# Two MLPs behind a Fourier transform: other steps give their squares and low parts to VectorE

## Chip, cores and metric

One core of a Trainium2 chip runs the whole program. The metric is the device time of one execution in microseconds (us). The kernel before was timed in 3 runs: median 1021.49 us, 1020.7 to 1024.02.

## The reference

```
X = fft(fft(x, axis=1), axis=2).real          # x: 2 x 3008 x 256
x = X.reshape(6016, 256)
h = x @ w_in;  g = relu(h) ** 2;  x = g @ w_out             # 256 -> 2048 -> 256
h = x @ w_in2; g = h * sigmoid(1.702 * h); out = g @ w_out2 # 256 -> 2048 -> 256
```

All inputs are float32. A float32 matrix product is made from three products of TensorE: each operand is split into a high part (a cast to the type fp32r) and a low part (the operand less its high part), and high x high, high x low and low x high are summed in PSUM.

## The kernel before, in words

The transform is folded by symmetry, so that the tokens come as 8 blocks (2 batches x 4 sets of frequencies) of 376 or 378 pairs; a pair is a frequency and its mirror. The features lie on the partitions. Names for the engines: PE is TensorE, DVE VectorE, ACT ScalarE, POOL GpSimd, SP the queue that issues all DMAs.

**The first MLP runs in 128 steps** (`steps`, the loop `for i in range(n)`). A step is one block and one group of 128 of the 2048 hidden features, and has these parts:

- `front1` (L468 to L470): 6 matmuls of 376 or 378 columns on TensorE into two PSUM tiles `psa`, an even and an odd part. Each of the two tiles has two buffers, so a step needs the tiles that were used two steps earlier.
- VectorE reads them: L727 makes `p` (even part plus a rank-one term), L729 and L730 make the two halves of `h`, sum and difference. L727 frees the even tile, L730 the odd one.
- the square of the relu of `h` (752 or 756 columns), in place. In a step of the set `SV` VectorE does it in one operation (L734); in any other step ScalarE does it in two, relu (L736) and square (L737).
- ScalarE casts `h` to its high part `gh` (L739).
- the low part `gl = h - gh`, a line of a helper (L76), one step later in the program: by VectorE if the step is in the set `VSTEPS`, else by GpSimd. `h` has 4 buffers, shared with the staging tiles `o` of outputs; `gh` and `gl` have 5.
- `back` (L483), four steps later (`LAG`): 12 matmuls from `gh`, `gl` and the output weights into two accumulators `psb`. At the end of a turn (4, 8 or 16 steps of a block) two copies (L596, one on ScalarE, one on VectorE) empty them into `o`, and a DMA stores it.

**Beside these, `background(i)` puts pieces of other work behind each step**, by the table `PLAN` (start, rate, due step): the weights of the first MLP are prepared (`conv`, up to step 36), further blocks of the transform folded, those of the second MLP prepared (`w2a`, steps 55 to 78, and `w2b`, 85 to 117), and the second MLP's first input read back (`y0`, from step 117). A group of weights (`widen`, `widen_in`, `narrow`) is turned from 64-bit words into float32 by L169 and L172 on ScalarE and L173, L174, L182, L183 and L185 on VectorE; ScalarE casts it (L208, L254), and VectorE or GpSimd (L76, and L246 for sums of the second MLP's) makes its low part. L173 needs L169, L183 needs L172 (or L182). L293 to L311 fold blocks of the transform. L620 adds parts of the second MLP's input on GpSimd.

**The order on each engine** is fixed when the program is built: a scheduler goes through the program with its own estimate of times and issues each engine's instructions in the order in which it expects them to be ready. Each engine then runs its list strictly in order and waits on semaphores. So a change of who makes a square moves other instructions too.

**The second MLP** (from `with tc.manual_schedule()`) is ordered by hand, in 64 units, and takes the second half of the time.

Of the kernel before, what the change touches and what calls it, by code (L numbers as in the profile page):

```python
# [42 lines left out]
THROTTLE = 18  # L43

LOW = {(0, 0, 0): "V", (0, 0, 1): "V", (0, 0, 2): "G", (0, 0, 3): "G", (0, 1, 0): "G", (0, 1, 1): "G", (0, 1, 2): "G", (0, 1, 3): "V", (1, 0, 0): "G", (1, 0, 1): "G", (1, 0, 2): "G", (1, 0, 3): "G", (1, 1, 0): "G", (1, 1, 1): "G", (1, 1, 2): "G", (1, 1, 3): "V"}
VSTEPS = {17, 23, 26, 28, 29, 34, 44, 45, 50, 60, 75, 76, 82, 89, 113}
RA = {(0, 0, 0), (0, 0, 1), (0, 0, 2), (0, 0, 3), (0, 1, 1), (0, 1, 2), (0, 1, 3), (1, 0, 1)}
EOG = {1, 2, 3}
SV = {3, 9, 13, 17, 19, 25, 34, 49, 51, 79, 80, 96}
LOWE = {(0, 0): "V", (0, 1): "G", (0, 2): "V", (0, 3): "V", (1, 0): "V", (1, 1): "G", (1, 2): "G", (1, 3): "V"}  # L50
FINE = set()
PARKED = ((0, 2), (1, 2), (0, 3), (1, 3))
# [11 lines left out]
def spectral_two_mlps_kernel(  # L64
# [10 lines left out]
    def sub(eng, o, a, b):  # L75
        eng.tensor_tensor(out=o, in0=a, in1=f32(b), op=ALU.subtract)  # L76
# [511 lines left out]
    def store(j, f):  # L588

        wd = WID[blocks[j][1]]  # L590
        y = dram.tile([P, 2, 2, NP], F32, tag=f"y{j}_{f}", name="ydram")
        ydram.setdefault(j, []).append(y)
        for ec in range(2):
            o = m.tile([P, 2, NP], F32, tag="h", name="o", bufs=4)
            ap = acc[j][ec][:, :, 0:wd]
            (A.copy, V.tensor_copy)[ec](o[:, :, 0:wd], ap)  # L596
            nc.sync.dma_start(y[:, ec, :, 0:wd], o[:, :, 0:wd])
# [103 lines left out]
    for i in range(n):  # L701
# [29 lines left out]
        if done and done[3]:  # L731
            store(*done[:2])
        if i in SV:
            V.scalar_tensor_tensor(out=hv, in0=hv, scalar=0.0, in1=hv, op0=ALU.max, op1=ALU.mult)  # L734
# [6 lines left out]
        def low_part(i, key, h, gh):  # L741
            pw = WID[blocks[key[0]][1]]
            gl = mg.tile([P, 2, NP], F32R, tag="gl", name="gl", bufs=5)
            sub(G if i not in VSTEPS else V, gl[:, :, 0:pw], h[:, :, 0:pw], gh[:, :, 0:pw])
            gst[key] = (gh, gl)
# [270 lines left out]
```

## Time and profile before

| | |
|---|---|
| median of 3 runs | 1021.49 us |
| the profiled execution: its time, its span | 1022.03 us, 1020.2 us |
| TensorE (PE) busy | 983.7 us, 96% |
| VectorE (DVE) busy | 816.6 us, 80% |
| ScalarE (ACT) busy | 612.9 us, 60% |
| GpSimd (POOL) busy | 354.6 us, 35% |
| relu (L736), square (L737), cast (L739) on ScalarE, mean of one | 832, 834, 821 ns |
| granted clock of TensorE, mean | 0.99 |

The span runs from the first instruction to the last. Busy shares are means over stages with different limits, so they are read by stretches. A busy TensorE is not at its peak: the ends of its matmuls are modelled, and they overlap (one takes 0.34 us and the next starts 0.17 us after it). The granted clock is the share of TensorE's full 2.4 GHz that it got. A number in brackets behind a row of the order of time is the engine's idle time before the row, with the instruction whose end released it.

### The profile page before, as it was taken

The numbers are of one execution on the slowest core, as the hardware profiler recorded it, in microseconds if no ns is written. First come the engines' busy times: TensorE is split into PE (matmuls) and PEld (weight loads), VectorE is DVE, ScalarE is ACT, GpSimd is POOL, SyncE is SP. The second block draws the span as 40 slices with busy tenths as digits, with TensorE's granted clock in tenths as the row PEclk, the third lists the DMA queues.
The fourth block names the chain that finished last, engine by engine and source line by source line (L and its number), as shares of the span: only waits on it lengthen the run. The fifth ranks groups of instructions, "written<-read, shape, count | busy, mean of one in ns | idle before, by whom it ended". The sixth has DMA issues, their size and how long they took to land.

```text
span 1020.2 us, 14245 instructions
## 1 busy us (share of the span) xinstructions
PE 983.7 (96%) x5582; PEld 948.6 (93%) x5582; DVE 816.6 (80%) x1089; ACT 612.9 (60%) x764; POOL 354.6 (35%) x216
## 2 busy tenths in 40 slices
PE   9989989899999999998899999999999999999998
PEld 9579978898999898898899999999999999999997
DVE  7996899885777598775678888888888888888874
ACT  2577666775888588687744454544545454454443
POOL 2447554643867449596605302002020020200000
PEclk9899999999999999899999999999999999999999
DMA  7531221201233021201441200000100000000000
GB/s 293 208 119 71 73 85 70 72 31 54 104 124 114 31 83 57 73 16 61 186 132 31 77 16 31 31 32 16 46 1 31 31 31 31 1 31 1 31 1 30
DMA packets 22914, 65.22 MB, mean 64 GB/s; under 512 B 1856, under 2 KB 14272, under 8 KB 19648
## 3 DMA queue, kind: packets, MB, share of 16 engines
q1 hardware_dynamic: 22848, 64.32, 17.7%
q8 instruction: 43, 0.70, 0.3%
q14 instruction: 23, 0.19, 0.1%
HBM read 43.13 MB, written 21.19 MB: 63 GB/s over the span
## 4 chain that ended last, share of the span: by engine, by line
PE 69%; DVE 16%; ACT 7%; issue 5%; POOL 1%; DMA 0%; DVEq 0%; ACTq 0%; POOLq 0%
PE psb L796 24%; PE psc L780 21%; PE psb L483 13%; PE psa L468 2%; PE psa L367 2%; ACT h L736 2%; PE psa L469 2%; PE psa L470 2%; DVE h L730 2%; DVE p L727 2%; DVE h L729 2%; ACT h L737 2%; DVE ue L183 1%; DVE gl L76 1%; PE psa L284 1%
## 5 line engine op out<-in xcount | busy, mean ns | idle before, releaser
L76 POOL TENSOR_TENSOR gl<-h,gh 128x752 fp32r<-128x752 f32 (+1 forms) x113 | 218.5, 1944 | 157.9 <-ACT gh L739 135.7
L483 PE MATMUL psb<-gh,w 128*128 128x376 f32 (+1 forms) x1024 | 241.6, 338 | 4.3 <-DVE o L596 4.3
L796 PE MATMUL psb<-gh,w 128*128 128x376 f32 (+1 forms) x1024 | 237.8, 334 | 0.0
L483 PEld LDWEIGHTS psb<-gh,w 128*128 128x128 f32 x1024 | 184.8, 191 | 6.0 <-DVE o L596 5.5
L796 PEld LDWEIGHTS psb<-gh,w 128*128 128x128 f32 x1024 | 182.9, 188 | 0.0
L736 ACT ACTIVATE h<-h 128x752 f32<-128x752 f32 (+1 forms) x116 | 96.2, 832 | 81.0 <-DVE h L730 75.8
L483 PE MATMUL psb<-gl,w 128*128 128x376 f32 (+1 forms) x512 | 132.2, 339 | 2.2 <-POOL gl L76 2.2
L861 ACT ACTIVATE g<-c 128x1128 f32<-128x1128 f32 (+1 forms) x64 | 73.7, 1152 | 99.5 <-DVE c L859 99.5
L796 PE MATMUL psb<-gl,w 128*128 128x376 f32 (+1 forms) x512 | 129.9, 335 | 0.4 <-DVE gl L76 0.3
L739 ACT CAST gh<-h 128x752 fp32r<-128x752 f32 (+1 forms) x128 | 104.7, 821 | 23.3 <-DVE h L734 16.2
L76 DVE TENSOR_TENSOR gl<-g,gh 128x1504 fp32r<-128x1504 f32 (+1 forms) x64 | 111.8, 1747 | 1.6 <-ACT gh L841 1.6
L630 POOL TENSOR_TENSOR ue<-raw 128x376 f32<-128x376 f32 (+1 forms) x16 | 18.4, 1174 | 271.4 <-DVE ya L76 271.2
L841 ACT CAST gh<-g 128x1504 fp32r<-128x1504 f32 (+1 forms) x64 | 93.1, 1454 | 31.4 <-DVE g L832 31.4
L727 DVE SCALAR_TENSOR_TENSOR p<-n,w1n_t,psa 128x376 f32<-128x376 f32 (+1 forms) x128 | 76.0, 600 | 41.6 <-PE psa L470 41.2
L468 PE MATMUL psa<-eo,w 128*128 128x376 f32 (+1 forms) x256 | 90.5, 355 | 16.9 <-DVE h L730 11.6
L737 ACT ACTIVATE h<-h 128x752 f32<-128x752 f32 (+1 forms) x116 | 96.4, 834 | 3.0
L483 PEld LDWEIGHTS psb<-gl,w 128*128 128x128 f32 x512 | 94.0, 191 | 2.5 <-POOL gl L76 2.5
L796 PEld LDWEIGHTS psb<-gl,w 128*128 128x128 f32 x512 | 92.1, 188 | 1.0 <-DVE gl L76 1.0
L832 DVE TENSOR_TENSOR g<-g,c 128x1128 f32<-128x1128 f32 (+1 forms) x64 | 89.8, 1403 | 1.2 <-ACT g L861 1.2
L858 DVE TENSOR_TENSOR g<-g,psc 128x376 f32<-128x376 f32 (+1 forms) x64 | 35.0, 547 | 69.0 <-ACT g L857 69.0
L469 PE MATMUL psa<-eo,w 128*128 128x376 f32 (+1 forms) x256 | 86.1, 337 | 0.0
L470 PE MATMUL psa<-eo,w 128*128 128x376 f32 (+1 forms) x256 | 85.8, 336 | 0.0
(139 smaller groups left out, 1625.6 us busy)
## 6 DMA issues: line engine op xcount, KB each, us to landing
ydram<-o SPq DMA_DIRECT2D x18, 376.0 KB, 2.9
xt<-in_x SPq DMA_DIRECT2D x5, 1024.0 KB, 6.9
cst<-in_dfts SPq DMA_DIRECT2D x8, 570.0 KB, 6.0
raw<-ydram SPq DMA_DIRECT2D x6, 752.0 KB, 4.6
out<-o SPq DMA_DIRECT2D x11, 376.0 KB, 3.1
raw<-in_w1i SPq DMA_DIRECT2D x4, 1024.0 KB, 5.4
raw<-in_w1o SPq DMA_DIRECT2D x4, 1024.0 KB, 6.5
raw<-in_w2i SPq DMA_DIRECT2D x4, 1024.0 KB, 4.9
```

The costliest lines, as they stand in the source:

```text
L76: eng.tensor_tensor(out=o, in0=a, in1=f32(b), op=ALU.subtract)
L468: T.matmul(o, lhsT=w[:, 0, fs], rhs=t[:, par, 0, 0:wd], start=True, stop=False)
L469: T.matmul(o, lhsT=w[:, 0, fs], rhs=t[:, par, 1, 0:wd], start=False, stop=False)
L470: T.matmul(o, lhsT=w[:, 1, fs], rhs=t[:, par, 0, 0:wd], start=False, stop=True)
L483: T.matmul(acc[j][ec][:, s, 0:wd], lhsT=w[:, hl, e0:e0 + P], rhs=(gh, gl)[gi][:, s, 0:wd], start=(first and hl == 0 and gi == 0), stop=(la ...
L727: V.scalar_tensor_tensor(out=p[:, 0:wd], in0=e128[blocks[j]][:, 0:wd], scalar=w1n_t[:, 0, f:f + 1], in1=ps[:, 0, 0:wd], op0=ALU.mult, op1= ...
L736: A.activation(out=hv, in_=hv, func=AF.Relu)
L737: A.activation(out=hv, in_=hv, func=AF.Square)
L739: last_a = A.copy(gh[:, :, 0:wd], hv)
L780: T.matmul(bank, lhsT=w[:, hl, slot * P:(slot + 1) * P], rhs=t[:, yl, i], start=(first and hl == 0 and yl == 0), stop=(hl == 1), skip_grou ...
L796: T.matmul(o[:, s, 0:wd], lhsT=w[:, hl, e0:e0 + P], rhs=g[:, 2 * i + s, 0:wd], start=(f == 0 and hl == 0 and g is gh), stop=(f == 15 and h ...
L841: A.copy(gh[:, :, 0:pw], g[:, :, 0:pw])
```

## The change

Two sets of step numbers are replaced. `SV`, the steps whose square VectorE makes, had 12 members and has 15; `VSTEPS`, those whose low part VectorE makes, had 15 and has 12. Up to step 43 both are now empty. Nothing else is edited.

```diff
-VSTEPS = {17, 23, 26, 28, 29, 34, 44, 45, 50, 60, 75, 76, 82, 89, 113}
+VSTEPS = {44, 45, 50, 58, 61, 72, 75, 82, 93, 96, 107, 110}
-SV = {3, 9, 13, 17, 19, 25, 34, 49, 51, 79, 80, 96}
+SV = {49, 51, 59, 60, 66, 73, 74, 79, 80, 94, 95, 101, 108, 109, 115}
```

The scheduler then orders the engines anew. Pieces of these orders follow, from steps 24 to 31 on three engines and from steps 115 to 118 on one. The numbers behind names tell tiles apart and differ between the two programs.

TensorE at step 30. The first row is the last front matmul of step 29; `psb` rows are the output matmuls of step 24, `psa_1392` (before) and `psa_1398` (changed) the even tile of step 30, `psa_1435` that of step 31. Before:

```order
L470 MATMUL psa_1345<-eo_304,w_871 128x378
L483 MATMUL psb_1352<-gh_1210,w_727 128x378 x2
L483 MATMUL psb_1352<-gl_1246,w_727 128x378 x2
L483 MATMUL psb_1352<-gh_1210,w_727 128x378 x2
L483 MATMUL psb_1353<-gh_1210,w_727 128x378 x2
L483 MATMUL psb_1353<-gl_1246,w_727 128x378 x2
L483 MATMUL psb_1353<-gh_1210,w_727 128x378 x2
```

With the change:

```order
L470 MATMUL psa_1351<-eo_304,w_874 128x378
L468 MATMUL psa_1398<-eo_304,w_874 128x378
L469 MATMUL psa_1398<-eo_304,w_874 128x378
L470 MATMUL psa_1398<-eo_304,w_874 128x378
L468 MATMUL psa_1435<-eo_304,w_874 128x378
L483 MATMUL psb_1358<-gh_1215,w_729 128x378 x2
L483 MATMUL psb_1358<-gl_1252,w_729 128x378 x2
```

Four front matmuls, of steps 30 and 31, now stand ahead of the output matmuls of step 24.

ScalarE in the same place, from the cast of the weights before (L208) to the first operations on the next weights (L169, L172). `h_1238` and `h_1269` are steps 25 and 26 before, `h_1243` and `h_1275` the same with the change. Before:

```order
L208 CAST w_1214<-ue_1114 128x1024
L739 CAST gh_1244<-h_1238 128x756
L736 ACTIVATE h_1269<-h_1269 128x756
L596 COPY o_1309<-psb_1077 128x2x376
L737 ACTIVATE h_1269<-h_1269 128x756
L736 ACTIVATE h_1303<-h_1303 128x756
L739 CAST gh_1276<-h_1269 128x756
L169 ACTIVATE ue_1280<-raw_1045 128x1024
L172 ACTIVATE ue_1280<-raw_1045 128x1024
```

With the change:

```order
L208 CAST w_1219<-ue_1119 128x1024
L736 ACTIVATE h_1243<-h_1243 128x756
L736 ACTIVATE h_1275<-h_1275 128x756
L737 ACTIVATE h_1243<-h_1243 128x756
L737 ACTIVATE h_1275<-h_1275 128x756
L739 CAST gh_1250<-h_1243 128x756
L739 CAST gh_1282<-h_1275 128x756
L169 ACTIVATE ue_1286<-raw_1050 128x1024
L172 ACTIVATE ue_1286<-raw_1050 128x1024
L596 COPY o_1315<-psb_1082 128x2x376
```

Relu and square of step 25 are added, and the copy of the accumulator (L596) has moved behind the weights' two operations.

VectorE in the same place: L596 empties an accumulator, `p_1332` and `p_1379` (before) and `p_1338` and `p_1385` (changed) are steps 28 and 29. Before:

```order
L596 COPY o_1312<-psb_1078 128x2x376
L727 SCALAR_TENSOR_TENSOR p_1332<-n_316,w1n_t_125,psa_1323 128x378
L727 SCALAR_TENSOR_TENSOR p_1379<-n_316,w1n_t_125,psa_1344 128x378
L76 TENSOR_TENSOR gl_1319<-h_1269,gh_1276 128x756
L729 TENSOR_TENSOR h_1331<-p_1332,psa_1324 128x378
L173 TENSOR_SCALAR ue_1280<-ue_1280 128x1024
L730 TENSOR_TENSOR h_1331<-p_1332,psa_1324 128x378
```

With the change:

```order
L727 SCALAR_TENSOR_TENSOR p_1338<-n_316,w1n_t_125,psa_1329 128x378
L173 TENSOR_SCALAR ue_1286<-ue_1286 128x1024
L727 SCALAR_TENSOR_TENSOR p_1385<-n_316,w1n_t_125,psa_1350 128x378
L596 COPY o_1318<-psb_1083 128x2x376
L174 TENSOR_SCALAR ue_1286<-ue_1286 128x1024
L729 TENSOR_TENSOR h_1337<-p_1338,psa_1330 128x378
L730 TENSOR_TENSOR h_1337<-p_1338,psa_1330 128x378
```

L173 of the weights has moved ahead of L727 of step 29, which frees the tile that the first matmul of step 31 needs.

GpSimd near the end of the first MLP: the low parts of steps 115 to 118 and the addition L620. Before:

```order
L76 TENSOR_TENSOR gl_4498<-h_4462,gh_4476 128x2x376
L620 TENSOR_TENSOR raw_4169<-raw_4169,ue_4546 128x1512
L76 TENSOR_TENSOR gl_4543<-h_4489,gh_4496 128x2x376
L76 TENSOR_TENSOR gl_4577<-h_4534,gh_4541 128x2x376
L630 TENSOR_TENSOR ue_4642<-raw_4169 128x378 x2
L630 TENSOR_TENSOR ue_4642<-raw_4169,ue_4642 128x378 x2
L76 TENSOR_TENSOR gl_4608<-h_4568,gh_4575 128x2x376
```

With the change:

```order
L76 TENSOR_TENSOR gl_4495<-h_4460,gh_4473 128x2x376
L76 TENSOR_TENSOR gl_4540<-h_4486,gh_4493 128x2x376
L620 TENSOR_TENSOR raw_4169<-raw_4169,ue_4543 128x1512
L76 TENSOR_TENSOR gl_4574<-h_4531,gh_4538 128x2x376
L630 TENSOR_TENSOR ue_4639<-raw_4169 128x378 x2
L630 TENSOR_TENSOR ue_4639<-raw_4169,ue_4639 128x378 x2
L76 TENSOR_TENSOR gl_4605<-h_4565,gh_4572 128x2x376
```

The low part of step 116 has moved ahead of L620.

## Rows read from the trace of the kernel before

**Rows 1.** By stretch: length; PE, PEld, DVE, ACT, POOL busy (us); clock; DMA share, GB/s.

```profile
20.00:120.00 100.00, 92.23 (x479) 77.59 (x478) 88.63 (x130) 63.63 (x81) 53.02 (x30) 0.97 0.37 126
120.00:210.00 90.00, 80.05 (x447) 74.75 (x446) 81.05 (x113) 65.70 (x84) 50.89 (x27) 1.00 0.22 74
210.00:400.00 190.00, 188.00 (x1073) 178.95 (x1073) 142.85 (x224) 142.24 (x186) 113.03 (x74) 1.00 0.20 74
400.00:500.00 100.00, 92.51 (x503) 89.98 (x502) 71.47 (x101) 76.01 (x100) 74.17 (x45) 0.95 0.19 71
...
400.00:420.00 20.00, 15.99 (x75) 15.01 (x74) 16.67 (x18) 12.48 (x17) 13.58 (x8) 0.83 0.26 91
```

**Rows 2.** TensorE's waits, 0 to 620 us: us in total, times, longest.

```profile
PE psa L468 <- DVE h L730: 11.6, 18, 1.4
PE psb L483 <- DVE o L596: 4.3, 4, 1.5
PE psa L468 <- DVE p L727: 4.2, 6, 1.3
```

**Rows 3.** TensorE in order of time: rows that begin with a wait.

```profile
73.62 0.44 PE L468 MATMUL psa<-eo,w 128*128 128x376 f32 x1 [1.09 <-DVE h L730]
76.50 0.61 PE L483 MATMUL psb<-gh,w 128*128 128x376 f32 x2 [1.06 <-DVE o L596]
89.88 0.61 PE L483 MATMUL psb<-gh,w 128*128 128x376 f32 x2 [0.63 <-DVE o L596]
119.30 0.44 PE L468 MATMUL psa<-eo,w 128*128 128x376 f32 x1 [0.65 <-DVE h L730]
...
145.46 0.61 PE L483 MATMUL psb<-gh,w 128*128 128x378 f32 x2 [1.08 <-DVE o L596]
153.89 0.44 PE L468 MATMUL psa<-eo,w 128*128 128x378 f32 x1 [1.39 <-DVE h L730]
...
163.91 0.44 PE L468 MATMUL psa<-eo,w 128*128 128x378 f32 x1 [0.38 <-DVE h L730]
...
183.67 0.44 PE L432 MATMUL psa<-eo,sel_t 128*128 128x376 f32 x1 [0.81 <-DVE eo L76]
...
292.58 0.44 PE L468 MATMUL psa<-eo,w 128*128 128x378 f32 x1 [0.35 <-DVE h L730]
...
407.37 0.61 PE L483 MATMUL psb<-gh,w 128*128 128x376 f32 x2 [1.49 <-DVE o L596]
...
414.04 0.68 PE L468 MATMUL psa<-eo,w 128*128 128x376 f32 x1 [1.26 <-DVE h L730]
...
478.20 1.00 PE L483 MATMUL psb<-gl,w 128*128 128x376 f32 x2 [2.23 <-POOL gl L76]
```

**Rows 4.** Durations (ns: min/median/max) of low parts and squares; ScalarE's square (sum, mean).

```profile
L76 DVE TENSOR_TENSOR gl<-h,gh x15: 929/940/1782, 108.1 to 460.9; 128x752 fp32r<-128x752 f32 x9, 128x756 fp32r<-128x756 f32 x6
L734 DVE SCALAR_TENSOR_TENSOR h<-h x12: 931/943/3059, 62.1 to 392.7; 128x752 f32<-128x752 f32 x8, 128x756 f32<-128x756 f32 x4
...
L76 POOL TENSOR_TENSOR gl<-h,gh x113: 1770/1828/2869, 42.9 to 507.1; 128x752 fp32r<-128x752 f32 x87, 128x756 fp32r<-128x756 f32 x26
...
L737 ACT ACTIVATE h<-h 128x752 f32<-128x752 f32 x88 | 73.2, 833 | 2.3
```

**Rows 5.** VectorE in order of time: start, us, instruction.

```profile
64.35 2.16 DVE L173 TENSOR_SCALAR ue<-ue 128x1024 f32<-128x1024 f32 x1
...
137.35 3.06 DVE L734 SCALAR_TENSOR_TENSOR h<-h 128x756 f32<-128x756 f32 x1
...
147.66 0.69 DVE L173 TENSOR_SCALAR ue<-ue 128x1024 f32<-128x1024 f32 x1
```

**Rows 6.** GpSimd in order of time, the low part of step 3.

```profile
64.13 1.82 POOL L76 TENSOR_TENSOR gl<-h,gh 128x756 fp32r<-128x756 f32 x1 [2.79 <-ACT gh L739]
```

**Rows 7.** VectorE in order of time, the weights' operation ahead of step 100.

```profile
408.58 2.83 DVE L183 SCALAR_TENSOR_TENSOR ue<-raw,ue 128x1024 uint32<-128x1024 uint32 x1
```

**Rows 8.** GpSimd in order of time, L620.

```profile
472.96 3.46 POOL L620 TENSOR_TENSOR raw<-raw,ue 128x1512 f32<-128x1512 f32 x1 [2.72 <-DMA ue<-ydram]
```

## Prediction

> **What bounds the kernel now.** I read the busy time by stretch first, then TensorE's waits, then each wait's place in the order of time. By stretch [rows 1], TensorE is busy 188.0 of 190 us between 210 and 400 us, so nothing is left to gain there. The second MLP, behind 510 us, is not touched by the change, and I carry it over. TensorE loses time in two places: 7.8 and 9.9 us idle in 20 to 120 and 120 to 210 us (counting L727 rows from the start, these hold steps 0 to 43), and 7.5 us in 400 to 500 us. There the granted clock is 0.95, which is 5 us more of full-speed time, 3.4 of them in 400 to 420 us, where it is 0.83 [rows 1]: for a while the clock is at 1.2 GHz instead of 2.4, each time after TensorE has waited.
>
> Who is waited for stands in [rows 2]: up to 620 us, TensorE's first matmul of a step waits 11.6 us for L730 and 4.2 us for L727 to free its PSUM tile, and the output matmuls 4.3 us for L596. All three run on VectorE, 20.1 us together. VectorE is busy 88.6 of 100 and 81.1 of 90 us in the first two stretches [rows 1], so in these it is nearly a bound; ScalarE (64 and 66 us) and GpSimd (53 and 51 us) have room. The waits there are many and short: [rows 3] shows the larger ones, from 0.63 to 1.39 us before 210 us.
>
> **The change part by part.** *Removed from VectorE up to step 43:* squares of 7 steps (3, 9, 13, 17, 19, 25, 34) and low parts of 6 (17, 23, 26, 28, 29, 34). One of either takes 0.94 us by the median and at most 3.06 and 1.78 [rows 4]. The least is 13 x 0.94 = 12.2 us; the long ones are those that meet a GpSimd operation. *Added:* 7 x (0.83 + 0.83) = 11.6 us of relu and square on ScalarE, 6 x 1.83 = 11.0 us on GpSimd [rows 4]. Both fit their room in sum, so the question is the order. Little of VectorE's saving lies on TensorE's path: where TensorE runs without a wait (steps 13 to 19), a square taken away buys nothing. I go from place to place.
>
> *Steps 5 to 12: +1.1 us.* Without the square of step 3, L173 of the weights starts before GpSimd's low part of that step. Before, it started 0.2 us behind it and took 2.16 us, against 0.69 where GpSimd rests [rows 5, 6]. So L730 of step 7 and the copy L596 come 2.5 us earlier, and of the 1.09 and 1.06 us at 73.6 and 76.5 us [rows 3] about 0.7 stays: 1.45 us, with the slow first matmul behind each wait 1.7. At 89.9 us the copy waits for the low part of step 9, whose square now runs on ScalarE: that wait of 0.63 grows to 1.2. Net 1.1.
>
> *Step 22: +0.7.* The 0.65 us at 119.3 [rows 3] follow the square of step 19, which is gone.
>
> *Steps 25 to 27: +1.6.* The square of step 25 took 3.06 us at 137.35 [rows 5], since GpSimd worked throughout; the low part of step 23 is gone as well. TensorE reaches step 28 about 3.4 us ahead of before.
>
> *Steps 28 to 31: -3.7, the term I am least sure of.* The order of TensorE changes: before, the output matmuls of steps 24 and 25 follow at once on step 29; now three matmuls of step 30 and one of step 31 come first, and that one needs the PSUM tile that L727 of step 29 frees. On VectorE that L727 now stands behind L173, which needs ScalarE's L169. ScalarE must first make two relus, two squares and two casts, six operations of 0.83 [rows 4], 5.0 us, from about 133.9 us (I put L730 of step 24 at 130.4, 2.2 us ahead of before; behind it come its relu, square and cast and a weights' cast of 1.0), so L169 (1.1 us) ends near 139.9. Then L173 meets GpSimd's low part of step 25, 139.7 to 141.5 by the same reckoning, and has to let it end, as at 64.35 us; L727 ends near 142.8. TensorE, done with its other work at 138.6, would idle 4.2 us. Before, it lost 1.9 us here in three waits, the last and longest 1.08 us [rows 3], and 0.3 in slow starts: net -2.0. The wait of 2.23 us at 478 us [rows 3] was followed by the low clock, which cost what the first one left of the 5.0, 1.6 us [rows 1]; I charge 1.7. Bounds: -0.3 (L173 slips in before GpSimd, the clock holds) and -6 (L169 late by 2 us more).
>
> *Steps 31 to 38: +3.7.* The 1.39 us at 153.9 [rows 3] follow the low parts of steps 26 and 28, both gone: 1.7 with slow starts. Of six waits from 163.9 to 183.7 us, 3.2 us together [rows 3], I take 2.0, as the square and low part of step 34 and the low part of step 29 (2.8 us) are no longer ahead of them; bounds 0 and 3.2.
>
> Sum up to step 43: 1.1 + 0.7 + 1.6 - 3.7 + 3.7 = 3.4 us gained.
>
> *After step 43* VectorE gets 11 squares (59, 60, 66, 73, 74, 94, 95, 101, 108, 109, 115) and loses one (96); it gets 7 low parts and loses 4 (60, 76, 89, 113): 13 more, at least 12.2 us. ScalarE gives back 10 x 1.66 us. I count a VectorE delay as hidden while L727 runs less than 3.2 us behind its matmuls: a step takes TensorE 18 matmuls of 0.17 us, 3.1, and a tile is wanted again two steps on, 6.2 us, less 1.2 for its own matmuls and 1.75 for the three reads of it. By that, steps 58 to 62 and 72 to 75 come close, but at no cost. *Step 66: -1.0:* its square stands before L729 of step 67, whose L730 TensorE waited for already (0.35 us at 292.6 [rows 3]); 0.94 us go straight to that wait. Bounds -1.9 and 0.
>
> *Steps 93 to 103: +1.9.* At 402 to 411 us VectorE made L182, L173, L174 and L183 while GpSimd worked off a backlog; L183 alone took 2.83 us [rows 7], and TensorE waited three times, 1.49, 1.26 and 1.26 us, up to 414 us [rows 3]. Now GpSimd has two low parts less (93 and 96), 3.7 us, and VectorE two squares and two low parts more and one square less, 3 us. I get L730 of step 100 1.4 us earlier and waits of 3.2 instead of 4.0 us, with slow starts 1.9 gained by the output matmuls of step 98. The 1.2 GHz stretch behind it, 3.4 us, I leave in. Bounds: -2 (the additions all delay) and +5.3 (the clock holds).
>
> *Steps 116 to 118: +1.4.* GpSimd's L620 (3.46 us, behind a transfer's landing at 473.0 [rows 8]) stood before the low part of step 116, for which TensorE waited 2.23 us at 478 [rows 3]. Now that low part comes first and fits the 2.7 us in which GpSimd waited for the transfer [rows 8]. But the work behind L620 is the same, so the low part of step 118 ends only 1.8 us earlier and TensorE waits some 1.7 us there: gain 2.2, or 0.5 if the clock falls again; I take the middle. Bounds 0.5 and 3.9.
>
> Sum: 3.4 - 1.0 + 1.9 + 1.4 = 5.7 us. The profiled execution took 1022.03 us (span 1020.2); the median of the runs is 0.54 lower. 1022.03 - 5.7 = 1016.3, or **1016 us** against the median of 1021.49.
>
> **A rule against it.** The trace shows that VectorE and GpSimd hold each other up: L173 took 2.16 us as a low part started 0.2 us before it [rows 5, 6], while ScalarE's and TensorE's operations keep their lengths. The Trainium skill says the same of these engines' shared port ("SBUF — State Buffer", Who interferes with whom: whichever starts first has it for the whole instruction) and warns that moving operations between the two might not help ("Perfetto Trace Analysis", Optimizing Scalar/DVE Operations). By that rule the six moved low parts would return what they save; the trace bears out the mechanism, not yet the size, and that is the third rival.
>
> **Rivals.** *VectorE was simply the bound.* All of TensorE's waits for it before 210 us go: the 20.1 us less 5.3 around 400 to 465 us and 2.0 between 280 and 390, so 12.8; with the 2.3 of the later terms 15.1 less: 1007. For it: 89 and 90% busy [rows 1]. Against: its order still holds bursts of four weights' operations, and L173 waits for ScalarE.
>
> *VectorE becomes the bound after step 43 (slower).* Of the 18 squares and low parts that are new there, each costs TensorE 0.94 us once L727 runs over 3.2 us behind its matmuls, as at step 66. If nine do, 8.5 us stand in place of the -1.0 and +1.9 above: 1022.03 + 8.5 - 3.4 - 1.4 = 1025.7, or 1025 by the median. The ninth is the one from which it can be told from no change. For it: GpSimd is busy 113 of 190 us there [rows 1], so a square may take up to the 3.06 us seen. Against: VectorE idles 47 of these 190 us [rows 1].
>
> *Nothing measurable.* GpSimd's 11 us more stop VectorE's weights' operations: 6 low parts x 0.9 us, half of one, are 5.4 us, which eat the gain: 1021.
>
> **Chances.** Forecast 0.50, own range 1012 to 1020; VectorE the bound 0.15; slower 0.13; nothing 0.22. A measurement of this kernel can tell 0.3%, 3.06 us: faster is below 1018.4, slower above 1024.6. Of the forecast's half, 0.38 lies below 1018.4; with the first rival and a little of the last, faster 0.55. Slower 0.14, the rest 0.31. The range runs from the first rival's 1007 to 1024, which leaves out most of the slower one and some beyond the first.
>
> **What would show it.** Right: no VectorE square or low part before step 44; TensorE's wait at 153 us gone; one wait of 3 to 5 us near 139 us followed by a lower clock; a new or longer wait at step 69; the wait for L620's follower moved from step 116 to 118 and under 2 us. Wrong: no wait near 139 us (then nearer 1011), or waits of TensorE for L730 between 260 and 400 us above 4 us in sum (then the slower case); or a clock below 0.9 in a new stretch.

## The result, and the profile after

| | before | after |
|---|---|---|
| median of 4 runs each, on one chip | 1021.33 us | 1012.01 us |
| ratio, with its 95% interval | | 0.9899 (0.9879 to 0.9919) |
| span of the profiled execution | 1020.2 us | 1009.5 us |
| TensorE, VectorE, ScalarE, GpSimd busy | 983.7, 816.6, 612.9, 354.6 us | 974.7, 817.7, 609.9, 366.7 us |
| mean granted clock | 0.99 | 0.996 |

The change made the kernel faster, by 10.3 us by the ratio (8.3 to 12.4). 1016 us had been predicted. VectorE is as busy as before in sum. By stretch (same columns and stretches as [rows 1]), profile after:

```profile
20.00:120.00 100.00, 92.73 (x506) 80.69 (x505) 83.67 (x130) 75.10 (x97) 58.53 (x32) 1.00 0.36 128
120.00:210.00 90.00, 84.13 (x481) 82.19 (x480) 77.50 (x113) 71.44 (x90) 58.50 (x34) 0.98 0.21 73
210.00:400.00 190.00, 184.37 (x1046) 174.53 (x1044) 152.89 (x224) 130.33 (x169) 117.30 (x74) 1.00 0.20 74
400.00:500.00 100.00, 92.74 (x516) 89.72 (x516) 75.62 (x110) 75.18 (x97) 74.13 (x43) 0.98 0.25 89
400.00:420.00 20.00, 17.36 (x98) 16.73 (x99) 17.09 (x25) 15.11 (x20) 12.80 (x7) 1.00 0.26 92
```

From 120 to 210 us TensorE is idle 5.9 us (9.9 before), from 210 to 400 us 5.6 us (2.0 before): the gain lies early, and a part is paid back in the middle. From 400 to 420 us the clock is 1.00, where it had been 0.83. TensorE's waits up to 620 us, for [rows 2]:

```profile
PE psa L468 <- DVE h L730: 8.2, 9, 2.5
PE psa L468 <- DVE p L727: 3.6, 4, 1.9
...
PE psb L483 <- DVE o L596: 0.9, 2, 0.6
```

The three groups that made 20.1 us now make 12.7. L730 is waited for 9 times instead of 18, but for up to 2.5 us. The rows that answer to [rows 3], TensorE in order of time:

```profile
139.24 0.44 PE L468 MATMUL psa<-eo,w 128*128 128x378 f32 x1 [1.95 <-DVE p L727]
141.46 0.83 PE L483 MATMUL psb<-gh,w 128*128 128x378 f32 x2 [0.63 <-DVE o L596]
171.71 0.44 PE L431 MATMUL psa<-eo,sel_t 128*128 128x376 f32 x1 [1.06 <-ACT eo L375]
173.71 0.44 PE L432 MATMUL psa<-eo,sel_t 128*128 128x376 f32 x1 [1.11 <-DVE eo L76]
184.07 0.44 PE L468 MATMUL psa<-eo,w 128*128 128x376 f32 x1 [0.98 <-DVE p L727]
283.14 0.44 PE L468 MATMUL psa<-eo,w 128*128 128x378 f32 x1 [0.90 <-DVE h L730]
285.61 0.44 PE L468 MATMUL psa<-eo,w 128*128 128x378 f32 x1 [1.15 <-DVE h L730]
382.11 0.44 PE L468 MATMUL psa<-eo,w 128*128 128x376 f32 x1 [2.48 <-DVE h L730]
407.81 0.44 PE L468 MATMUL psa<-eo,w 128*128 128x376 f32 x1 [1.53 <-DVE h L730]
475.61 0.61 PE L483 MATMUL psb<-gl,w 128*128 128x376 f32 x2 [2.03 <-POOL gl L76]
```

Between 64 and 128 us only 0.06 us is left of the four waits of 0.63 to 1.09. At 139 us stands the foreseen stop. From 150 to 206 us ten waits of 6.7 us became the three of 171.71 to 184.07, 3.15 us. The waits at 283, 285 and 382 us are new or longer; the one for GpSimd's low part has moved from step 116 to 118. VectorE's answer to the first of [rows 5] is this row of after: L173 starts ahead of GpSimd's low part and takes 0.68 us, not 2.16.

```profile
64.23 0.68 DVE L173 TENSOR_SCALAR ue<-ue 128x1024 f32<-128x1024 f32 x1
```

### The profile page after: what moved, and what is told of

Its sections match the earlier page's. It is cut to its first block, busy times and chain, and to the rows that moved or that the text cites. A ratio compares the mean times of both kernels' runs of the same rounds, so it can differ in the third digit from the quotient of the medians.

```text
span 1009.5 us, 14240 instructions
## 1 busy us (share of the span) xinstructions
PE 974.7 (97%) x5582; PEld 943.8 (93%) x5582; DVE 817.7 (81%) x1089; ACT 609.9 (60%) x758; POOL 366.7 (36%) x219
## 4 chain that ended last, share of the span: by engine, by line
PE 69%; DVE 15%; ACT 7%; issue 5%; POOL 3%; DMA 1%; SPq 0%; DVEq 0%; ACTq 0%; POOLq 0%
PE psb L796 25%; PE psc L780 23%; PE psb L483 12%; PE psa L367 2%; ACT h L736 2%; PE psa L468 2%; ACT h L737 2%; DVE p L727 2%; PE psa L470 2%; DVE h L729 2%; PE psa L469 2%; DVE h L730 2%; POOL gl L76 1%; ACT gh L739 1%; DVE gl L76 1%
## 5 line engine op out<-in xcount | busy, mean ns | idle before, releaser
L76 POOL TENSOR_TENSOR gl<-h,gh 128x752 fp32r<-128x752 f32 (+1 forms) x116 | 224.9, 1944 | 139.2 <-ACT gh L739 108.6
L483 PE MATMUL psb<-gh,w 128*128 128x376 f32 (+1 forms) x1024 | 240.4, 338 | 2.4 <-ACT o L596 1.4
L483 PEld LDWEIGHTS psb<-gh,w 128*128 128x128 f32 x1024 | 183.6, 190 | 4.3 <-ACT o L596 2.0
L736 ACT ACTIVATE h<-h 128x752 f32<-128x752 f32 (+1 forms) x113 | 93.9, 832 | 74.5 <-DVE h L730 73.4
L483 PE MATMUL psb<-gl,w 128*128 128x376 f32 (+1 forms) x512 | 131.3, 337 | 2.0 <-POOL gl L76 2.0
L727 DVE SCALAR_TENSOR_TENSOR p<-n,w1n_t,psa 128x376 f32<-128x376 f32 (+1 forms) x128 | 76.2, 599 | 31.8 <-PE psa L470 31.7
L737 ACT ACTIVATE h<-h 128x752 f32<-128x752 f32 (+1 forms) x113 | 94.0, 834 | 3.0
L483 PEld LDWEIGHTS psb<-gl,w 128*128 128x128 f32 x512 | 93.4, 190 | 2.4 <-POOL gl L76 2.3
```

Of the source, the lines that this page charges most:

```text
L483: T.matmul(acc[j][ec][:, s, 0:wd], lhsT=w[:, hl, e0:e0 + P], rhs=(gh, gl)[gi][:, s, 0:wd], start=(first and hl == 0 and gi == 0), stop=(la ...
L727: V.scalar_tensor_tensor(out=p[:, 0:wd], in0=e128[blocks[j]][:, 0:wd], scalar=w1n_t[:, 0, f:f + 1], in1=ps[:, 0, 0:wd], op0=ALU.mult, op1= ...
L736: A.activation(out=hv, in_=hv, func=AF.Relu)
L737: A.activation(out=hv, in_=hv, func=AF.Square)
```

## The experiments

I call **lead** how much earlier, from the span's start, the first output matmul of a step (L483) starts than in the profile of before. It tells where time is won and lost, in us; a lead of 9.0 that falls to 7.0 has lost 2. What it is at step 3 is chance of the start, where the change does not show yet, so what has been won by a step is the lead there less that of step 3. Leads come from one profiled execution each, the ratios from all runs of a kernel against those of before.

| kernel | step 3 | 14 | 45 | 60 | 90 | 103 | 119 | 126 | ratio, 95% interval |
|---|---|---|---|---|---|---|---|---|---|
| the change | -0.7 | 2.4 | 8.9 | 8.9 | 6.9 | 9.0 | 8.8 | 11.2 | 0.9899 (0.9879 to 0.9919) |
| early part alone | -0.2 | 2.9 | 5.6 | 5.6 | 5.1 | 7.8 | 5.3 | 4.8 | 0.9924 (0.9902 to 0.9946) |
| late part alone | -0.2 | 1.5 | 1.4 | 1.4 | -0.7 | 1.2 | 0.0 | 1.3 | 0.9991 (0.9975 to 1.0006) |
| 7 early squares | -1.0 | 2.1 | 4.9 | 4.9 | 4.9 | 6.4 | 5.3 | 4.5 | 0.9944 (0.9925 to 0.9962) |
| 6 early low parts | -0.8 | 0.9 | 0.1 | 0.1 | 0.0 | 1.2 | -0.8 | -0.9 | 1.0016 (0.9999 to 1.0032) |
| these and square 34 | -1.4 | 0.3 | 2.8 | 2.8 | 2.8 | 4.1 | 2.1 | 2.0 | 0.9977 (0.9962 to 0.9992) |
| square 34 alone | -0.3 | 1.4 | 3.6 | 3.5 | 3.6 | 4.7 | 5.0 | 4.7 | 0.9979 (0.9963 to 0.9994) |
| change, square 34 back | -0.4 | 2.7 | 4.7 | 4.7 | 2.2 | 4.2 | 4.2 | 6.5 | 0.9952 (0.9933 to 0.9972) |
| change, square 26 added | -0.3 | 2.8 | 3.0 | 3.0 | 0.7 | 2.7 | 2.5 | 3.3 | 0.9972 (0.9957 to 0.9986) |
| change, 4 squares added | -0.9 | 2.2 | 5.0 | 1.3 | -0.7 | 1.1 | 0.9 | 1.8 | 0.9978 (0.9962 to 0.9994) |
| change, no square 66 | -0.2 | 2.9 | 9.3 | 9.3 | 8.1 | 10.2 | 10.3 | 10.1 | 0.9907 (0.9887 to 0.9927) |
| change, late from step 72 | -0.1 | 3.0 | 5.8 | 5.8 | 5.4 | 7.4 | 8.8 | 8.4 | 0.9915 (0.9890 to 0.9939) |
| change, low part 92 for 93 | -0.6 | 2.5 | 9.0 | 9.0 | 7.0 | 10.4 | 11.7 | 11.6 | 0.9912 (0.9889 to 0.9935) |

**The early part alone, and the late part alone.** The first against the change, the second against the kernel before:

```diff
-VSTEPS = {44, 45, 50, 58, 61, 72, 75, 82, 93, 96, 107, 110}
+VSTEPS = {44, 45, 50, 60, 75, 76, 82, 89, 113}
-SV = {49, 51, 59, 60, 66, 73, 74, 79, 80, 94, 95, 101, 108, 109, 115}
+SV = {49, 51, 79, 80, 96}
```

```diff
-VSTEPS = {17, 23, 26, 28, 29, 34, 44, 45, 50, 60, 75, 76, 82, 89, 113}
+VSTEPS = {17, 23, 26, 28, 29, 34, 44, 45, 50, 58, 61, 72, 75, 82, 93, 96, 107, 110}
-SV = {3, 9, 13, 17, 19, 25, 34, 49, 51, 79, 80, 96}
+SV = {3, 9, 13, 17, 19, 25, 34, 49, 51, 59, 60, 66, 73, 74, 79, 80, 94, 95, 101, 108, 109, 115}
```

> Only the members up to step 43 leave the two sets (13 operations taken from VectorE); from step 44 on the sets are those of the kernel before. My theory: nearly the whole gain is made up to step 43, because the lead of the changed kernel over the kernel before is 9.6 us when TensorE leaves step 43. Then this kernel leads by 9.6 us there, keeps its stops near 413 and 478 us as before, and takes 1011 to 1014 us. Rival 1 (the steps added after step 43 free GpSimd and ScalarE and make half of the gain): about 1016.5. Rival 2 (the late additions cost what the early lead gained beyond the measured 9.3 us): below 1009.

> The sets keep the members of the kernel before up to step 43 and take those of the changed kernel from step 44 on. My theory: the late part is nearly neutral, its own terms by the lead step by step being -1.7 (step 66), +2.0 (steps 91 to 103) and about 0 (steps 116 to 119), so 1019 to 1022 us. Rival 1 (half of the gain is late): about 1016.5. Rival 2 (the late additions cost): 1024 or more.

Early 0.9924 is 7.8 us less, late 0.9991 is 0.9 less with an interval that holds 0. The theory stands on where the gain lies, but its 9.6 us of lead did not come, and its 1011 to 1014 us was a little low (median 1015.12). The lead at step 45 shows more: the early part alone and the changed kernel are **the same program up to 257 us**, instruction by instruction on every engine, and yet one profile leads by 5.6 us there and the other by 8.9. Where they part: two stretches (columns as in [rows 1]) of the changed kernel, the same of the early part alone, and TensorE's rows of the early part alone.

```profile
141.00:145.00 4.00, 3.54 (x12) 3.57 (x13) 4.00 (x5) 2.21 (x4) 3.31 (x2) 0.58 0.37 136
...
172.00:180.00 8.00, 6.89 (x43) 6.69 (x43) 6.76 (x11) 5.13 (x8) 3.01 (x3) 1.00 0.00 0
```

```profile
141.00:145.00 4.00, 4.00 (x23) 4.00 (x24) 4.00 (x5) 2.18 (x4) 2.85 (x2) 1.00 0.26 97
172.00:180.00 8.00, 6.88 (x26) 6.75 (x25) 4.70 (x7) 4.15 (x6) 2.21 (x2) 0.57 0.00 0
```

```profile
138.76 0.44 PE L468 MATMUL psa<-eo,w 128*128 128x378 f32 x1 [1.96 <-DVE p L727]
140.97 0.58 PE L483 MATMUL psb<-gh,w 128*128 128x378 f32 x2 [0.65 <-DVE o L596]
...
171.25 0.44 PE L431 MATMUL psa<-eo,sel_t 128*128 128x376 f32 x1 [2.37 <-ACT eo L375]
173.25 0.68 PE L432 MATMUL psa<-eo,sel_t 128*128 128x376 f32 x1 [1.12 <-DVE eo L76]
...
199.04 0.44 PE L468 MATMUL psa<-eo,w 128*128 128x376 f32 x1 [0.65 <-DVE p L727]
201.31 0.44 PE L468 MATMUL psa<-eo,w 128*128 128x376 f32 x1 [0.98 <-DVE h L730]
```

The stop near 139 us is the same to 0.02 us in both. In one execution 1.2 GHz follows it, in the other not. The one that keeps its clock comes 1.3 us sooner to L431, for which ScalarE's cast is no sooner ready, so it waits 2.37 us instead of 1.06; and then 1.2 GHz follows there, for longer. So more was lost at 172 us than had been kept at 141: at step 39 the two are 1.1 us apart. The rest of the 3.3 us comes with the waits at 199 and 201 us, which the changed kernel's profile does not have. All six kernels with this early program show one course or the other: a lead at step 45 of 8.9, 9.3 and 9.0 us with 1.2 GHz from 141 us, or of 5.6, 5.8 and 5.0 with 1.2 GHz from 172 us. Executions of a single kernel spread as far: of the six of the change with the late part from step 72, three took 1010.4 to 1011.5 us and three 1014.6 to 1016.0.

Likewise the late part alone has the early program of before, and yet won 1.7 us by step 14. VectorE's and GpSimd's rows near 68 us, first of the kernel before, then of the late part alone:

```profile
67.86 2.23 DVE L174 TENSOR_SCALAR ue<-ue 128x1024 uint32<-128x1024 uint32 x1
...
67.70 1.84 POOL L76 TENSOR_TENSOR gl<-h,gh 128x752 fp32r<-128x752 f32 x1 [1.75 <-ACT gh L739]
```

```profile
67.90 0.68 DVE L174 TENSOR_SCALAR ue<-ue 128x1024 uint32<-128x1024 uint32 x1
...
67.94 2.34 POOL L76 TENSOR_TENSOR gl<-h,gh 128x752 fp32r<-128x752 f32 x1 [1.94 <-ACT gh L739]
```

GpSimd 0.16 us ahead: VectorE's L174 takes 2.23 us. VectorE 0.04 us ahead: 0.68, and GpSimd's takes 2.34. The three other kernels with the program of before up to step 14 (low parts alone, these and square 34, square 34 alone) have 0.68 us too and win the same 1.7 us, so it is the profile of before that is the odd one, and every lead from step 14 on contains 1.7 us of that. So a profile of this kernel carries up to 3 us of chance by step 45, and a term below that, read from one pair of profiles, is not yet the change's.

**Squares alone, low parts alone** (against the kernel before):

```diff
-SV = {3, 9, 13, 17, 19, 25, 34, 49, 51, 79, 80, 96}
+SV = {49, 51, 79, 80, 96}
```

```diff
-VSTEPS = {17, 23, 26, 28, 29, 34, 44, 45, 50, 60, 75, 76, 82, 89, 113}
+VSTEPS = {44, 45, 50, 60, 75, 76, 82, 89, 113}
```

> Of the change only the seven squares up to step 43 leave VectorE; the low parts of all steps and the squares from step 44 on are those of the kernel before. My theory: by the places where the lead grew, steps 5 to 17 (+3.2), step 22 (+1.0) and half of steps 25 to 27 (+0.9) belong to squares, steps 31 to 45 (+5.8) to low parts but for the square of step 34; so a gain of 5 to 6 us: about 1016. Rival (each of the 13 operations is worth the same, 0.7 us): 7 x 0.7 = 5, also 1016, but then the gain is spread evenly and not in these places. Rival 2 (GpSimd's six more low parts stop VectorE's other operations, so that the squares alone are better than both): 1012 or less.

> Of the change only the six low parts up to step 43 move from VectorE to GpSimd; all squares and the low parts from step 44 on are those of the kernel before. My theory: the gain lies in steps 31 to 45, the waits near 153 us and from 163 to 184 us going: 3 to 5 us, about 1017. Rival (GpSimd's operations hold up VectorE's, so a low part moved there gives back what it saves): 1021 to 1022, no gain.

The squares gain 5.7 us, as both readings had it. The low parts gain nothing (1.6 us more, 0.1 less to 3.3 more): my 3 to 5 us fell. The waits near 153 us went, but new ones came: 2.85 us up to 144.8 us and this, ScalarE's and TensorE's rows with the low parts alone:

```profile
171.03 0.82 ACT L739 CAST gh<-h 128x756 fp32r<-128x756 f32 x1 [5.32 <-DVE h L734]
...
178.31 0.81 ACT L375 CAST eo<-ue 128x752 fp32r<-128x752 f32 x1
```

```profile
179.17 0.68 PE L431 MATMUL psa<-eo,sel_t 128*128 128x376 f32 x1 [3.63 <-ACT eo L375]
```

ScalarE idles 5.32 us for VectorE's square of step 34, with everything behind it in its list, up to the cast L375 for which TensorE then waits. That one square was tested three ways.

**The square of step 34**: back in the changed kernel; gone beside the low parts; gone alone (the last two against the kernel before).

```diff
-SV = {49, 51, 59, 60, 66, 73, 74, 79, 80, 94, 95, 101, 108, 109, 115}
+SV = {34, 49, 51, 59, 60, 66, 73, 74, 79, 80, 94, 95, 101, 108, 109, 115}
```

```diff
-VSTEPS = {17, 23, 26, 28, 29, 34, 44, 45, 50, 60, 75, 76, 82, 89, 113}
+VSTEPS = {44, 45, 50, 60, 75, 76, 82, 89, 113}
-SV = {3, 9, 13, 17, 19, 25, 34, 49, 51, 79, 80, 96}
+SV = {3, 9, 13, 17, 19, 25, 49, 51, 79, 80, 96}
```

```diff
-SV = {3, 9, 13, 17, 19, 25, 34, 49, 51, 79, 80, 96}
+SV = {3, 9, 13, 17, 19, 25, 49, 51, 79, 80, 96}
```

> The changed kernel, with the square of step 34 on VectorE again, as before the change; the orders of TensorE and GpSimd stay the same. My theory: TensorE's waits of 1.06 to 2.37 us for L375 near 170 us come from ScalarE, which has relu, square and cast of steps 33 and 34 ahead of L375; without two of these L375 comes up to 1.7 us earlier, the wait for it goes and with it the lower clock behind it in some runs: 1 to 3 us less, 1009 to 1011. Rival (ScalarE's list is in order, so its cast of step 34 waits for VectorE's square, as in the run of the low parts alone, where ScalarE idled 5.32 us for a square of VectorE at 171 us): L375 comes later, the wait for it is 3 us or more, and the time is 1014 to 1016.

> The six low parts up to step 43 on GpSimd and the square of step 34 on ScalarE; the six other early squares (3, 9, 13, 17, 19, 25) stay on VectorE, and all of step 44 on is as before. With the square of step 34 on VectorE the low parts alone gained nothing (ratio 1.0016). My theory: the low parts are worth some 3 us, which the in-order wait of ScalarE for that square (5.32 us idle, then 3.63 us of TensorE for L375) ate; so without it 0.997, about 1018.5 us. Rival (the low parts gain nothing because GpSimd's longer work holds up VectorE, or because the squares left ahead still set the pace): 1.000 or above, 1021 to 1023.

> The kernel before with one number less: the square of step 34 goes to ScalarE, all else as before the change. Put back into the changed kernel that square cost 5.4 us (ratio 0.9952 against 0.9899), and taken out beside the low parts it gained 3.9 (0.9977 against 1.0016). My theory: it is the dearest of the 13, since ScalarE idles behind it (5.2 us for a square of 2.56 us) with the cast L375 of the next block in its list: 3 to 5 us gained, ratio 0.995 to 0.997, about 1017.5 us, with TensorE's waits from 163 to 184 us (3.2 us in the kernel before) smaller. Rival (the square is dear only once the others are gone, because in the kernel before TensorE reaches L431 6 us later and ScalarE's cast is ready by then): the ratio is 0.999 to 1.001.

Put back it costs 5.4 us (0.9952 against 0.9899): my theory fell, the rival is right. VectorE's, GpSimd's, ScalarE's and TensorE's rows with it back:

```profile
163.79 2.56 DVE L734 SCALAR_TENSOR_TENSOR h<-h 128x756 f32<-128x756 f32 x1
```

```profile
163.55 2.00 POOL L76 TENSOR_TENSOR gl<-h,gh 128x756 fp32r<-128x756 f32 x1
```

```profile
166.45 0.82 ACT L739 CAST gh<-h 128x756 fp32r<-128x756 f32 x1 [5.20 <-DVE h L734]
...
173.71 0.81 ACT L375 CAST eo<-ue 128x752 fp32r<-128x752 f32 x1
```

```profile
174.58 0.68 PE L431 MATMUL psa<-eo,sel_t 128*128 128x376 f32 x1 [3.63 <-ACT eo L375]
```

The orders of TensorE and GpSimd are those of the changed kernel, so this is the square's doing: ScalarE is spared 1.66 us of work but idles 5.20 us there instead of 1.80, L375 starts at 173.71 instead of 170.84 us, and TensorE loses 2.6 us more there, with 1.2 GHz from 174 to 181 us.

Gone beside the low parts it gains 4.0 us. That is near the time of the theory (0.9977, 0.997 expected), but not for its reason: the low parts beside it bring nothing either way (0.9977 against 0.9979). Gone alone it gains 2.1 us (0.6 to 3.8), between theory and rival. The waits from 163 to 184 us did not get smaller, as I had expected: five of them, 3.5 us, stand in place of six of 3.2. Of three waits behind them, 2.04 us in the kernel before, 0.28 is left. TensorE with that square alone gone:

```profile
178.64 0.44 PE L431 MATMUL psa<-eo,sel_t 128*128 128x376 f32 x1 [0.93 <-ACT eo L375]
...
189.92 0.44 PE L468 MATMUL psa<-eo,w 128*128 128x376 f32 x1 [0.28 <-DVE p L727]
```

The square's length differs as well. In the changed kernel with the square back, it starts 0.24 us behind a low part of GpSimd and takes 2.56 us. In the kernel before, GpSimd is idle there (172.1 to 178.0 us), the square takes 0.93 us, and ScalarE idles 3.62 us for it. VectorE and ScalarE before:

```profile
172.29 0.93 DVE L734 SCALAR_TENSOR_TENSOR h<-h 128x756 f32<-128x756 f32 x1
```

```profile
173.32 0.82 ACT L739 CAST gh<-h 128x756 fp32r<-128x756 f32 x1 [3.62 <-DVE h L734]
```

So what an edit is worth seems to depend on which others are made (2.1, 4.0 and 5.4 us). The traces give a reason; by the times alone it is not shown, as the intervals of the first and the last overlap.

**One more square, and four more** (against the changed kernel):

```diff
-SV = {49, 51, 59, 60, 66, 73, 74, 79, 80, 94, 95, 101, 108, 109, 115}
+SV = {26, 49, 51, 59, 60, 66, 73, 74, 79, 80, 94, 95, 101, 108, 109, 115}
```

```diff
-SV = {49, 51, 59, 60, 66, 73, 74, 79, 80, 94, 95, 101, 108, 109, 115}
+SV = {46, 47, 49, 51, 53, 54, 59, 60, 66, 73, 74, 79, 80, 94, 95, 101, 108, 109, 115}
```

> The changed kernel with one more square on VectorE, that of step 26. ScalarE then has four operations instead of six ahead of the weights' L169, TensorE runs the output matmuls of steps 24 to 26 ahead of step 30's front again, and L173 stands a step earlier. My theory: the stop at 137 to 141 us (1.95 and 0.63 us, and the lower clock from 141.6 to 145.0 us that followed it in the profile of the changed kernel) shrinks to under 1 us; 1.5 to 3.3 us less, ratio 0.987 to 0.988. Rival (a square of VectorE that meets GpSimd's low parts takes up to 3.06 us, as that of step 25 did, and holds L727 up): the stop stays or grows, ratio 0.990 to 0.993.

> The changed kernel with four more squares on VectorE, of steps 46, 47, 53 and 54: there TensorE runs without a wait from 193 to 282 us, and no weights are prepared between steps 37 and 54. My theory: what an added square costs depends on its place; one of step 34 cost 5.4 us and one of step 26 7.4 us, but these four cost nothing: ratio 0.990 (0.988 to 0.993), and no new wait of TensorE between 205 and 250 us. Rival (each operation on VectorE costs the same, 9.3 us for 13, 0.7 us each): 2.9 us more, ratio 0.993, with waits for L730 there. Rival 2 (squares are dear wherever they lie): 10 us more or worse, ratio 1.000.

Both theories fell. The square of step 26 costs 7.5 us, in the way of the rival, whose 3 us at most were too few. ScalarE's L169 did come 1.65 us sooner (134.97 us), but VectorE and GpSimd with that square:

```profile
136.13 2.83 DVE L173 TENSOR_SCALAR ue<-ue 128x1024 f32<-128x1024 f32 x1 [0.78 <-ACT ue L169]
139.00 2.16 DVE L174 TENSOR_SCALAR ue<-ue 128x1024 uint32<-128x1024 uint32 x1
```

```profile
136.04 2.37 POOL L293 TENSOR_TENSOR t<-xt 128x1024 f32<-128x1024 f32 x1
```

L173 now starts 0.09 us behind GpSimd's L293 and takes 2.83 us; in the changed kernel it slipped in ahead of a low part (0.89 us). TensorE waits 1.45 and 2.90 us there.

The four squares of steps 46, 47, 53 and 54, where TensorE had no wait, cost 8.1 us by the ratio. VectorE, GpSimd and TensorE with them:

```profile
220.49 2.55 DVE L734 SCALAR_TENSOR_TENSOR h<-h 128x752 f32<-128x752 f32 x1
...
228.23 0.93 DVE L596 COPY o<-psb 128x752 f32<-128x752 f32 x1
```

```profile
220.40 1.84 POOL L76 TENSOR_TENSOR gl<-h,gh 128x752 fp32r<-128x752 f32 x1 [2.06 <-ACT gh L739]
```

```profile
230.41 0.44 PE L468 MATMUL psa<-eo,w 128*128 128x376 f32 x1 [1.89 <-DVE zc L336]
```

Of the rivals, 2.9 us is too little; 10 us or more is nearer, but the loss that the trace shows comes from one place, and not from squares wherever they lie. The squares of 46 and 47 make VectorE late, so that the square of step 49, which was there before, starts 0.09 us behind a low part of GpSimd and takes 2.55 us instead of 0.93. L596 and L336 of the turn's end follow late, TensorE waits 1.89 us, and the clock falls (0.66 from 230 to 235 us). That is the lead's fall from 5.0 to 1.3. It accounts for 3.7 of the 8.1 us; how much of the rest is the worse of the two courses up to step 45, which this profile took, the timed runs can't tell. From step 49 to 60, past the squares of steps 53 and 54, the lead does not fall further.

**Three late places** (against the changed kernel): no square of step 66; steps 58 to 66 as before; the low part of step 92 in place of 93.

```diff
-SV = {49, 51, 59, 60, 66, 73, 74, 79, 80, 94, 95, 101, 108, 109, 115}
+SV = {49, 51, 59, 60, 73, 74, 79, 80, 94, 95, 101, 108, 109, 115}
```

```diff
-VSTEPS = {44, 45, 50, 58, 61, 72, 75, 82, 93, 96, 107, 110}
+VSTEPS = {44, 45, 50, 60, 72, 75, 82, 93, 96, 107, 110}
-SV = {49, 51, 59, 60, 66, 73, 74, 79, 80, 94, 95, 101, 108, 109, 115}
+SV = {49, 51, 73, 74, 79, 80, 94, 95, 101, 108, 109, 115}
```

```diff
-VSTEPS = {44, 45, 50, 58, 61, 72, 75, 82, 93, 96, 107, 110}
+VSTEPS = {44, 45, 50, 58, 61, 72, 75, 82, 92, 96, 107, 110}
```

> The changed kernel without the square of step 66 on VectorE (ScalarE makes it). My theory: this one square costs the two waits of 0.90 and 1.15 us at 282 to 286 us, against one of 0.35 us in the kernel before; both profiled kernels that hold it (the changed one and the late part alone) lost 1.7 us there. Without it the waits go back to one of about 0.35 us and the time falls by 1.7 us, ratio to the kernel before about 0.988, near 1010.3 us beside the changed kernel's 1012. Rival (what is lost there is won back at a later wait, since ScalarE gets 1.66 us of work): the waits at 282 us go, but the ratio stays at 0.990.

> The changed kernel, but for steps 58 to 66, which are as before the change: squares 59, 60 and 66 on ScalarE, low parts 58 and 61 on GpSimd, 60 on VectorE. My theory: the two waits of 0.90 and 1.15 us at 282 to 286 us are a backlog of VectorE from step 58 on, of which the square of step 66 is only the last part (without it alone 0.89 and 0.34 us stayed); so both give way to one of 0.35 us, and TensorE keeps 1.7 us more there: ratio 0.988, 1010 us, if it isn't lost again. Rival (what is not lost there is lost at the next wait, as after the run without the square of step 66, or costs nothing measurable): 0.990.

> The changed kernel with the low part of step 92 on VectorE in place of that of step 93; TensorE's order is the same. In the changed kernel GpSimd's low part of step 92 starts at 378.25 us, 0.15 us ahead of VectorE's L185 (378.40), which takes 2.74 us instead of the 1.21 of the kernel before, where the two start within 0.01 us of each other and VectorE goes first; TensorE then waits 2.48 us against 0.99. My theory: without that low part on GpSimd L185 takes 1.2 to 1.3 us and the wait at 379 us falls to about 1 us: 1.5 us gained at step 96 in the trace, and 0.988 to 0.990 by the runs, too little to tell by these alone. Rival (the wait comes from VectorE's list in sum, L182 to L185 and two squares, not from who starts first): the wait stays at 2 us or more, and L185 at 2.7.

By the ratios none differs from the change (0.9907, 0.9915, 0.9912), so none is shown to be better. The traces answer the questions of mechanism. Without the square of step 66 the waits are 0.89 and 0.34 us, so the square alone did not make both, and the theory of that run fell. With steps 58 to 66 as before they are one of 0.35, with nothing lost there. So the backlog begins at step 58, as the second theory said; its 1.7 us do not show in the time. For the third, VectorE's and then GpSimd's row of the changed kernel, and VectorE's and TensorE's of the variant:

```profile
378.40 2.74 DVE L185 CUSTOM_DVE_ANT_0 ue<-ue 128x2048 uint16<-128x2048 uint16 x1
```

```profile
378.25 1.81 POOL L76 TENSOR_TENSOR gl<-h,gh 128x752 fp32r<-128x752 f32 x1 [1.37 <-ACT gh L739]
```

```profile
378.34 1.21 DVE L185 CUSTOM_DVE_ANT_0 ue<-ue 128x2048 uint16<-128x2048 uint16 x1
```

```profile
380.52 0.45 PE L468 MATMUL psa<-eo,w 128*128 128x376 f32 x1 [0.94 <-DVE h L730]
```

With that low part gone from GpSimd L185 takes 1.21 us and the wait 0.94 instead of 2.48: that low part was the cause, and not VectorE's list in sum. Overlap alone is not enough: in the kernel before, GpSimd's low part and L185 start at 385.33 and 385.34 us, too close to tell which came first, and there L185 takes 1.21 us and the low part 2.87. Of the gain 1.4 us are there in the lead at step 103, and drown in the spread of the runs.

## Why the prediction was right, and where it wasn't

The sign, the range and the main place (up to step 43) were right; the size was short by 4 us. That the measured 1012.01 us lies within my own range of 1012 to 1020, by 0.01 us, is luck. So is the sum of the late terms, 2.3 us, as much as the lead grew from step 45 to 126: of its parts one is not the change's. Term by term:

- **Steps 5 to 12, +1.1.** The pair of profiles shows +3.1 by step 14. The four kernels with the early program of before have +1.7 of that, so the change's own part is 1.4. The size was about right, the working not: the wait of 0.63 at 89.9 us, which was to grow to 1.2, shrank to 0.06, and the delay of L174 counted as caused by the square of step 3 was chance of that one profile.
- **Step 22, +0.7:** +1.0. **Steps 25 to 27, +1.6:** +1.8 by the start of step 28.
- **Steps 28 to 31, -3.7:** -2.2 in the profile after, -0.7 in that of the early part alone. The stop is where it was put and for the reason given, L727 behind L173 behind L169. But it is 1.95 and 0.63 us, not 4.2. ScalarE's six operations began at 132.15 us instead of 133.9 and took 4.5 us instead of 5.0, so L169 ended at 137.7 us, not 139.9; and L173 got in 0.29 us ahead of GpSimd's low part, the bound that I had named and not taken. The run with the square of step 26 shows the course that I had taken: L173 behind an operation of GpSimd, and 4.6 us of lead lost. The clock, taken as 1.7 us, fell in one course and not in the other.
- **Steps 31 to 38, +3.7: the term that was most mis-sized in the profile after,** +5.9 from the stop to step 45 (+0.6 in the other course). The waits that I had counted, the one at 153.9 us and the six behind it, gave 4.2 us. What I had put at nothing are three waits of the kernel before that come next:

```profile
193.33 0.44 PE L468 MATMUL psa<-eo,w 128*128 128x376 f32 x1 [0.95 <-DVE p L727]
...
204.44 0.71 PE L328 MATMUL psa<-dft,xt 128*128 128x130 f32 x4 [0.44 <-DVE h L730]
205.80 0.44 PE L468 MATMUL psa<-eo,w 128*128 128x376 f32 x1 [0.65 <-DVE p L727]
```

They are gone in the profile after, and the lead grows by 1.7 us there; why was not traced. Nor had I seen what could take the term back. I had counted the square of step 34 as 0.94 us of VectorE's time. From step 33 to 39 the lead falls by 4.2 us where VectorE makes that square beside GpSimd's six low parts (low parts alone; change, square 34 back), and by 0.3 to 0.4 where ScalarE makes it (the change; these and square 34). In the other course of the early program it falls by 3.1 to 3.2.

- **Sum up to step 43, +3.4:** 7.8 us by the runs of the early part alone (5.5 to 10.0). Its profile shows 5.9 and that of the change 9.6, 1.7 of either from the profile of before.
- **Step 66, -1.0:** -1.7, within its bounds. The sentence that steps 58 to 62 come "close, but at no cost" was wrong: of the two waits one is theirs.
- **Steps 93 to 103, +1.9:** the lead rose by 2.1 us from step 90 to 103, and that isn't the change's. The early part alone, with the late sets of before, rose by 2.8 and the low parts alone by 1.2, because the profile of before was the one with 6.8 us of 1.2 GHz at 413 us. Among profiles without 1.2 GHz there the change's 2.1 stand against these 2.8; among those with half as long a stretch of it, 1.8 to 2.1 with the new late sets stand against 1.1 to 1.5. The change's own part is near nothing: shorter waits near 400 us, and 1.5 us lost at 382.
- **Steps 116 to 118, +1.4:** nothing by step 119 in the profile after (8.4 us of lead at the start of step 116, 8.7 at that of step 127). The wait moved as foreseen, but it is 2.03 us, not under 2, the clock falls behind it as before, and the time is the same. It is below my own lower bound of 0.5. Not foreseen were +2.5 us near 500 us, where TensorE waits 2.23 us for L836 instead of 3.18 and keeps its clock. The two places belong together. Of the eight kernels with late sets like the change's, six have 1.2 GHz behind the first wait, win 0.1 to 0.5 us there and wait 2.2 to 2.3 us for L836. Two (late from step 72, low part 92) keep the clock, win 1.8 and 1.7 us and then wait 3.7. Over both places, from step 114 to 127, the eight win 1.5 us in the mean and the six with the sets of before 0.1. So the size was about right, and a part of the 2.5 us is chance.

Of the rivals, the first did not come in full: of its 12.8 us of waits for VectorE before 210 us, 4.5 are left, and those for L730 behind are longer. The third had a true half: six low parts moved from VectorE to GpSimd gain nothing measurable alone, and the rows above show VectorE held up behind GpSimd by some 1.5 us or more in one place after the other. The Trainium skill ("SBUF — State Buffer", Who interferes with whom) has it that the order of issue and not the kind of operation decides which of them is blocked; L174, L173, L185 and the squares above agree. The squares, which went to ScalarE, gain 5.7 us alone; the 7.8 us of both are more, but the two intervals overlap. That VectorE would become the bound late did not come true, though my own mark for it did: TensorE's waits for L730 between 260 and 400 us come to 4.9 us, over the 4 I had set, and the lead falls by 3.5 us there (8.9 at step 60, 5.4 at step 93).

## What to carry to other kernels

Where engines run fixed lists, an operation is not worth its own length but what waits behind it in every list that it touches: look for an engine that is off the bound and idles long for one operation (5.2 us here for a square of 2.56), and try to move that one. One square shows it here. Before crediting an edit with a microsecond or two from a pair of profiles, look at a kernel whose program is the same up to that place. And a stop removed may only be met again at the next thing that isn't ready, so count a gain where the next long wait ends, not where it begins.

## What the runs showed of the hardware

- Two executions whose programs are the same up to 257 us stood 3.3 us apart at step 45: 1.2 GHz followed a stop of 1.95 and 0.63 us in one and not one of 1.96 and 0.65 us in the other. The Trainium skill ("TensorE: Matmul & The Clock Gate", Part 1) calls the number of slow matmuls at a kernel's start variable from run to run; these rows show the like in mid-kernel.
- A start that is 0.04 to 0.24 us sooner or later decides between VectorE and GpSimd: L174 0.68 or 2.23 us, L173 0.68 to 2.83, L185 1.21 or 2.74, a square 0.93 or 2.55. The bare length of such an operation is no price for it where GpSimd is at work.
